# Second pass, last layer: sums loaded into a unit's own tile, split there and stored from it

## The chip, the cores and the metric

The kernel runs on one core of one Trainium2 chip. The metric is the time of one execution in microseconds (us) of device time. Three runs of the kernel before took 1361.62, 1360.89 and 1360.49 us, median 1360.89.

## The reference

The program is an attention without softmax, followed by two layers of dense products. For each of 8 batches and 8 heads it forms kv = kᵀv (64 by 64) over 576 rows, then q·kv, divides each row by its root mean square and multiplies it by a gain. The 4608 tokens by 512 features that come out go through

```
h = x @ w_in                               # 512 -> 2048
x = softplus(h) @ w_out                    # 2048 -> 512
h = max(x @ w1, x @ w2, x @ w3)            # three times 512 -> 768
out = h @ w2_out                           # 768 -> 512
```

Everything is float32.

## The kernel before

The tokens are worked on in five passes of 2 x 456 or 2 x 464 tokens (`NS`). A product in float32 is made of three float32r products (`mm3`, L153 to L157): operand and weight are each split into a high part (a cast) and a low part (the value less the high part), and high·high, high·low and low·high are summed in PSUM. From the second pass on a block of products is multiplied by a seven-product scheme in the manner of Strassen and Winograd (`SLOT`, `ORDER`, products m = 1 to 7), for which sums and differences of weight blocks are needed. The first pass multiplies plainly; beside that it joins the raw weights, forms those sums on GpSimd, and stores what the later passes load. There are groups H (first layer), X (second), three times three groups for the third layer, and the last layer with 42 blocks of three matmuls (`OUT_SEQ`), e for the half of the output columns, m for the product, c for the chunk.

Weights come to TensorE as units: a tile `u` of 128 x 1024 (512 KB) that holds a high and a low half. There are `U_BUFS` = 4 such buffers, and 2 of half the size, `u3`. The first unit of a group has a buffer of its own, `ux` (`unit_tile` with `own`); from the third pass on there are two of these, used in turn by the count of the list `uxs`. A unit of the last layer serves four blocks, 12 matmuls; there are 11 (`OUT_UNITS`), the last half as big.

Not all units are split in the first pass. For the groups 23 and 24 (`LATE`) and for the last layer only the sums are stored. In the second pass, from 3 to 94 units of planned time after its start, 19 items (8 of the groups, 11 of the last layer) go one after the other through `load_sums` (a load of 256 KB into `st`, 2 buffers), `split_ahead` (ScalarE casts, GpSimd or VectorE subtracts, into `ahead` tiles, 4 buffers shared with k and v) and `keep_ahead` (two stores). Afterwards `load_unit` loads them as any other unit, in the second pass too.

The order of the work is set by planned times: `at(t, ...)` collects events, which are sorted by time and traced in this order; a planner then orders the engines' instructions. In the passes one and two, and around each start of a pass, `pinned` holds the order of the DMA queue of SyncE (SP, which issues all the loads and stores in question) to the order of the events. That queue works in order: a load that waits for its buffer holds up all that is behind it. `LEAD` = 10 is the planned time by which a unit is loaded ahead. One unit of planned time is about 1.25 us.

The attention of the next pass lies beside the third layer (`attention_beside`): k and v of a batch are loaded by `load_kv` for four pairs of heads. The first pass is opened by `OPENING`, a list written by hand in which the order on all engines is fixed: `r2.7` is the second refinement step of pair 7 (VectorE, it releases a PSUM bank), `jb.2.0` joins a weight (VectorE), `hc.0.1.1` casts an activation and `cc.1.0` a pair of weight blocks (both ScalarE).

Of the kernel before, what the change touches and what calls it, by code (L numbers as in the profile page):

```python
# [8 lines left out]
F32 = mybir.dt.float32  # L9
# [6 lines left out]
B, H, S, D = 8, 8, 576, 64  # L16
NT, DM, DFF, DF2 = B * S, H * D, 2048, 768
P = 128
# [25 lines left out]
LEAD = 10  # L44
# [5 lines left out]
ss.4:Y ra.0.1:cv LW.1.0 o.6:W rs.5 ja.0.1 xh.3 mm.7 t.5:p r1.5 LW.1.1 sq.6 jb.0.1 xl.3:p rs.4 r2.5 LW.2.0 ev.7:a  # L50
r1.4 o.7:X ra.1.0:cv t.4:p r3.5 rb.1.0 ss.6:Y wc.0.1:p sq.7 H.0.0.0:X r2.4 s1.0 rs.6 ja.1.0 ra.1.1:at t.6:p r1.6
ra.2.0:at wl.0.1:p jb.1.0 cc.0.1:a ss.7:Y rb.2.0 r2.6 LW.2.1 SA.0 wc.1.0:a cl.0.1 ja.2.0 H.0.1.0:Y rs.7 r3.4
wl.1.0:p xh.5 SB.0 t.7:a jb.2.0 SC.0.1 xh.4 r2.7 LW.8.0 tab wc.2.0:p r1.7 H.1.0.0:Y r3.6 SA.1 ra.2.1:cv wl.2.0:p
r3.7 sp.0.0.0 xh.6 xl.5:v hc.0.0.0:a xl.4:p H.2.0.0:X xh.7 hl.0.0.0 rb.2.1 xl.7:p s2.0 s3.0 SA.2 xl.6:v sp.0.1.0
rb.8.0 ja.2.1 s4.0 H.0.0.1:X hc.0.1.0:a jb.2.1 sp.2.0.0 cc.0.2:p rb.1.1 hl.0.1.0 cl.0.2 LW.8.1 hc.2.0.0:a ja.1.1
H.2.0.1:Y ra.8.0:cv hl.2.0.0 cc.0.0:p sp.0.0.1 ja.8.0 SC.0.2 cl.0.0 sp.1.0.0 jb.1.1 LW.9.0 hc.0.0.1:a hc.1.0.0:v
ra.8.1:at s1.1 H.1.0.1:X jb.8.0 LW.9.1 wc.1.1:a cc.1.1:a hl.1.0.0 wl.1.1:p SC.0.0 sp.2.0.1 hl.0.0.1 rb.8.1
cl.1.1 H.0.1.1:X hc.2.0.1:a ja.8.1 sp.1.0.1 s2.1 hl.2.0.1 wc.2.1:a SB.1 jb.8.1 s3.1 hc.1.0.1:a SC.1.1 wl.2.1:v
wc.8.1:a H.1.1.1:Y s4.1 cc.1.0:a wl.8.1:v sp.0.1.1 cl.1.0 cc.1.2:a hl.1.0.1 hc.0.1.1:a SB.2 cl.1.2 s1.2 s2.2
s3.2 s4.2 s1.8 s2.8 s3.8 s4.8 H.2.1.0:X hl.0.1.1 sp.1.1.1 SB.8 hc.1.1.1:v SC.1.0 hl.1.1.1 H.1.1.0:X SC.1.2  # L60
sp.2.1.0 ra.9.0:cv rb.9.0 hc.2.1.0:v hl.2.1.0 ja.9.0 jb.9.0 H.2.1.1:X sp.1.1.0 ra.9.1:W wc.8.0:a hc.1.1.0:v
hl.1.1.0 wl.8.0:v sp.2.1.1 rb.9.1 hc.2.1.1:v hl.2.1.1 ja.9.1 jb.9.1 SA.8
# [5 lines left out]
def kernel(  # L68
# [12 lines left out]
    nc = tc.nc  # L81
# [50 lines left out]
    for s in range(2):  # L132
        hi = const.tile([P, NP, P], F32R, name=f"kvh{s}")
        lo = const.tile([P, NP, P], F32R, name=f"kvl{s}")
        kvs.append((hi, lo))

    def cast(eng, hi, src):
        if eng is nc.scalar:
            nc.scalar.copy(hi, src)  # L139
        else:  # L140
            eng.tensor_copy(hi, src)  # L141

    def split(eng_hi, src, hi, lo, eng_lo):
        cast(eng_hi, hi, src)
        eng_lo.tensor_tensor(out=lo, in0=src, in1=hi.bitcast(F32), op=ALU.subtract)  # L145
# [34 lines left out]
    def at(t, fn, *args):  # L180
        events.append((t, len(events), fn, args))
# [11 lines left out]
    wd, units, st = {}, {}, {}  # L193
    uxs = []

    def unit_tile(size, p, own=False):
        if own and "ge" in pools:
            uxs.append(pools["ux"] if "ux" in pools and len(uxs) % 2 else pools["ge"])
            return uxs[-1].tile([P, 2, 512], F32R, tag="ux", bufs=1, name="ux")
        if size == 2:  # L200
            return up.tile([P, 2, 512], F32R, tag="u", bufs=U_BUFS, name="u")
        return up.tile([P, 1, 512], F32R, tag="u3", bufs=U3_BUFS, name="u3")

    def keep(key, u):
        n = u.shape[1] * 512
        wd[key] = dr.tile([P, n], F32, tag=f"wd{len(wd)}", name=f"wd{len(wd)}")
        nc.sync.dma_start(out=wd[key], in_=u.rearrange("p i n -> p (i n)").bitcast(F32))
# [13 lines left out]
    def load_sums(key, c0, n):  # L221
        t = pools["st"].tile([P, 512], F32, tag="st", bufs=2, name="st")
        st[key] = t[:, 0:n]
        nc.sync.dma_start(out=st[key], in_=wd["o" if key[0] == "o" else ("s", key[0])][:, c0:c0 + n])

    staged = {}

# [6 lines left out]
        staged[key] = (hi, lo)  # L234

    def keep_ahead(key, size):
        n, i = 256 * size, 1 if key[0] == "o" else size
        hi, lo = staged.pop(key)
        wd[key] = dr.tile([P, 2 * n], F32, tag=f"wd{len(wd)}", name=f"wd{len(wd)}")
        dst = wd[key].rearrange("p (i h n) -> p i h n", i=i, h=2)  # L240
        for h, t in enumerate((hi, lo)):
            nc.sync.dma_start(out=dst[:, :, h], in_=t.rearrange("p (i n) -> p i n", i=i))
# [56 lines left out]
    OUT_UNITS = [(4 * i, min(4, len(OUT_SEQ) - 4 * i)) for i in range(-(-len(OUT_SEQ) // 4))]  # L299
# [383 lines left out]
    def new_batches(pas, t):  # L683

        a = TOK[pas] + t * NS[pas]
        first = -1 if a == 0 else (a - 1) // S
        return list(range(first + 1, (a + NS[pas] - 1) // S + 1))

    def attention_beside(pas, t0):

        n = NS[pas]

        for t, start in ((0, t0 - 2), (1, t0 + 25.1)):
            tile = gc_tile if t or pas == 1 else partial(ge_tile, pas - 1)
            for b in new_batches(pas, t):
                for p in range(NP):
                    at(start - (12.5, 11, 16, 14.5)[p], load_kv, b, p, False, tile if p > 1 else None)
                at(start, kv_mm, b)
                at(start + (1.25 if t else 0.1), kv_evict, b)
        for k in range(2 * NP):  # L700
            h, p = divmod(k, NP)
            a = TOK[pas] + h * n
            t = t0 + 8 + 6 * k
            at(t - (12 if pas == 1 else 6 if k else 10), load_q, a, n, p)
            at(t - 3, split_q, a, n, p)
            at(t + 0.3, out_mm, a, n, p)
            at(t + 0.4, square, a, n, p)
            at(t + 4.8, ssq_mm, a, n, p, "W" if pas == 1 else "at")
            at(t + 4.9, root, a, n, p)
            at(t + (5.5 if pas == 1 else 4.9), norm, a, n, p)  # L710
# [3 lines left out]
    def run_pass(pas, base):  # L714
# [37 lines left out]
        start = {name: base + 7 * i for i, name in enumerate(order)}  # L752
# [8 lines left out]

        if pas == 1:
            ahead = [((g, k), 256 * PLACE[ms[0]], len(ms)) for g in range(LATE, G_O[0]) for k, ms in enumerate(UNITS)]
            ahead += [(("o", i // 4), i * P, n // 2) for i, n in OUT_UNITS]
            for i, (key, c0, size) in enumerate(ahead):
                t = base + 3 + 91 / len(ahead) * i
                at(t, load_sums, key, c0, 256 * size)
                at(t + 5, split_ahead, key, size)
                at(t + 8, keep_ahead, key, size)
# [26 lines left out]
        for fp in range(8):  # L796
            t = start[f"H{fp}"]
# [19 lines left out]
        for n in range(4):  # L817
            if pas == 0:
                for q in range(2):
                    t = start[f"X{n}{q}"]  # L820
# [10 lines left out]
            for q in range(2):  # L831
                t = start[f"X{n}{q}"]
# [58 lines left out]
        for k in range(9):  # L891
            fp, j = divmod(k, 3)
            t = base2 + 7 * k
# [16 lines left out]
        if pas + 1 < NPASS:  # L910
            attention_beside(pas + 1, base2)
            for s, ms in enumerate(STEPS):
                at(base3 + 5 + SLOT[ms[-1]] + 0.5, combine_x, pas + 1, (s,))
# [69 lines left out]
        t = base3 + 2.05  # L983
# [2 lines left out]
            return base3 + 23  # L986
        for i, n in OUT_UNITS:
            key, size, ti = ("o", i // 4), n // 2, t + 0.5 * i
            at(ti - (6 if i == 0 else LEAD), load_unit, pas, key, size, i == 0)
        for i, b in enumerate(OUT_SEQ):  # L990
            at(t + 0.5 * i, out_block, *b)
# [113 lines left out]
    for n, step in enumerate(OPENING):  # L1105
        name, _, opt = step.partition(":")
        kind, *index = name.split(".")
        t = OPEN + 0.25 * n
# [12 lines left out]
    base, bases = 0, []  # L1121
    for pas in range(NPASS):
        bases.append(base)
        base = run_pass(pas, base)
# [105 lines left out]
```

## Time and profile before

| | us |
|---|---|
| runs, median (range) | 1360.89 (1360.49 to 1361.62) |
| the profiled execution | 1361.93 |
| its span, first to last instruction | 1360.1 |
| TensorE (PE) busy in it | 1348.6 |
| VectorE, ScalarE, GpSimd busy | 819.0, 735.8, 650.9 |

The execution is 1.8 us longer than its span; that part lies outside the instructions. Times in the trace count from the span's start. PE, DVE, ACT, POOL and SPq are TensorE, VectorE, ScalarE, GpSimd and SyncE's queue; PEld are weight loads. Matmuls overlap, so that a duration of 0.37 us stands beside a distance from start to start of 0.21 us.

### The profile page before, as it was taken

The page shows a single profiled execution, that of the slowest core. Times are in us where ns is not written, and L with a number is a line of the kernel's source. Part 1 is how long each engine was busy: PE and PEld are TensorE (multiplying, and loading weights), DVE is VectorE, ACT ScalarE, POOL GpSimd, SP SyncE. Part 2 cuts the span into 40 slices and gives each one's busy share as a digit, 9 for nine tenths or more (in the row PEclk, how much of TensorE's full clock was granted, in tenths as well). Part 3 has the DMA queues.
Part 4 walks back from the last instruction along what each step waited for, and adds up shares of the span by engine and source line. Part 5 has one row for each costly group of instructions (what it writes and reads, how often), then busy time and mean ns, then how long its engine had stood idle before and what let it go on. Part 6 is the DMA issues. An engine that isn't in the chain of part 4 may idle for free.

```text
span 1360.1 us, 20399 instructions
## 1 busy us (share of the span) xinstructions
PE 1348.6 (99%) x6956; PEld 1196.6 (88%) x6956; DVE 819.0 (60%) x1301; ACT 735.8 (54%) x1426; POOL 650.9 (48%) x612
## 2 busy tenths in 40 slices
PE   9999999999999999999999999999999999999998
PEld 6899999998888888888888888888889889998897
DVE  6856758883545767735555676445567754447544
ACT  6776657873755456456444564554356546443332
POOL 6866545665554534345335354444434444336320
PEclk9999999999999999999999999999999999999999
DMA  8799889777999776586678765766766576666665
GB/s 294 240 324 348 263 299 342 260 251 239 330 318 313 253 283 238 183 306 209 203 240 274 239 207 189 279 208 205 245 199 213 175 282 217 216 213 190 226 200 172
DMA packets 135543, 336.12 MB, mean 247 GB/s; under 512 B 14608, under 2 KB 41104, under 8 KB 135440
## 3 DMA queue, kind: packets, MB, share of 16 engines
q1 hardware_dynamic: 134864, 333.90, 72.9%
q8 instruction: 56, 0.92, 0.3%
q10 hardware_dynamic: 576, 0.92, 0.2%
q14 instruction: 47, 0.39, 0.1%
HBM read 269.35 MB, written 65.40 MB: 246 GB/s over the span
## 4 chain that ended last, share of the span: by engine, by line
PE 95%; DMA 2%; DVE 1%; ACT 1%; POOL 1%; issue 0%; SPq 0%; POOLq 0%; ACTq 0%
PE Xo L155 6%; PE Xo L156 6%; PE Xo L157 6%; PE Xx L155 5%; PE Xx L157 5%; PE Xx L156 5%; PE Xh L155 5%; PE Xh L157 5%; PE Xh L156 5%; PE Yo L155 3%; PE Yo L156 3%; PE Yo L157 3%; PE Yx L155 3%; PE Yx L156 3%; PE Yx L157 3%; PE Yh L155 3%
## 5 line engine op out<-in xcount | busy, mean ns | idle before, releaser
L145 POOL TENSOR_TENSOR lo<-e,hi 128x464 fp32r<-128x464 f32 (+1 forms) x160 | 188.8, 1213 | 174.8 <-ACT hi L139 161.0
L139 ACT CAST hi<-t 128x464 fp32r<-128x464 f32 (+1 forms) x120 | 65.6, 547 | 124.5 <-DVE e L151 50.5
L155 PE MATMUL Xo<-hi,u 128*128 128x464 f32 (+1 forms) x296 | 110.8, 376 | 0.5 <-ACT m L139 0.4
L156 PE MATMUL Xo<-lo,u 128*128 128x464 f32 (+1 forms) x296 | 109.9, 371 | 0.0
L157 PE MATMUL Xo<-hi,u 128*128 128x464 f32 (+1 forms) x296 | 109.7, 371 | 0.0
L148 DVE TENSOR_TENSOR x<-x,Xx 128x464 f32<-128x464 f32 (+1 forms) x104 | 65.6, 632 | 60.1 <-PE Xx L157 59.8
L155 PE MATMUL Xh<-hi,u 128*128 128x464 f32 (+1 forms) x266 | 99.7, 375 | 1.4 <-DVE h L141 0.7
L157 PE MATMUL Xh<-hi,u 128*128 128x464 f32 (+1 forms) x266 | 98.8, 371 | 0.0
L156 PE MATMUL Xh<-lo,u 128*128 128x464 f32 (+1 forms) x266 | 98.6, 371 | 0.0
L139 ACT CAST hi<-e 128x464 fp32r<-128x464 f32 (+1 forms) x160 | 86.4, 580 | 22.0 <-PE Yx L156 16.7
L139 ACT COPY m<-Xo 128x464 f32<-128x464 f32 (+1 forms) x108 | 58.6, 547 | 70.1 <-PE Xo L157 67.6
L145 DVE TENSOR_TENSOR lo<-t,hi 128x464 fp32r<-128x464 f32 (+1 forms) x120 | 75.9, 636 | 33.3 <-ACT hi L139 29.0
L155 PE MATMUL Xx<-hi,u 128*128 128x464 f32 (+1 forms) x256 | 95.4, 372 | 0.1
L157 PE MATMUL Xx<-hi,u 128*128 128x464 f32 (+1 forms) x256 | 95.0, 371 | 0.0
L156 PE MATMUL Xx<-lo,u 128*128 128x464 f32 (+1 forms) x256 | 94.8, 370 | 0.0
L151 POOL TENSOR_TENSOR e<-e 128x464 f32<-128x464 f32 (+1 forms) x32 | 38.1, 1191 | 107.1 <-DVE t L151 89.7
L145 POOL TENSOR_TENSOR u<-sw,u 128x256 fp32r<-128x256 f32 (+1 forms) x67 | 67.8, 1027 | 32.8 <-ACT u L139 27.8
L145 POOL TENSOR_TENSOR lo<-m,hi 128x464 fp32r<-128x464 f32 (+1 forms) x40 | 47.8, 1213 | 74.6 <-ACT hi L139 74.6
L139 ACT CAST u<-sw 128x512 fp32r<-128x512 f32 (+1 forms) x120 | 62.8, 540 | 37.6 <-POOL sw L151 17.1
L148 DVE TENSOR_TENSOR Wh<-h,Wh 128x464 f32<-128x464 f32 (+1 forms) x32 | 20.6, 644 | 95.6 <-PE Wh L157 79.9
L151 POOL TENSOR_TENSOR sw<-sw 128x256 f32<-128x256 f32 x84 | 66.7, 797 | 23.7 <-DVE sw L280 19.6
L663 POOL TENSOR_TENSOR og<-og,r 128x464 f32<-128x464 f32 (+1 forms) x32 | 40.4, 1263 | 68.7 <-DVE r L659 48.1
(260 smaller groups left out, 4100.6 us busy)
## 6 DMA issues: line engine op xcount, KB each, us to landing
u<-wd SPq DMA_DIRECT2D x241, 512.0 KB, 4.4
ux<-wd SPq DMA_DIRECT2D x99, 512.0 KB, 3.5
wd<-u SPq DMA_DIRECT2D x161, 256.0 KB, 4.8
u<-wd SPq DMA_DIRECT2D x104, 256.0 KB, 4.0
raw<-in_w_out_dram SPq DMA_DIRECT2D x22, 512.0 KB, 4.9
raw<-in_w_dram SPq DMA_DIRECT2D x18, 512.0 KB, 5.5
raw<-in_w_in_dram SPq DMA_DIRECT2D x16, 512.0 KB, 5.5
wd<-ahead SPq DMA_DIRECT2D x32, 256.0 KB, 6.0
```

The costliest lines, as they stand in the source:

```text
L139: nc.scalar.copy(hi, src)
L145: eng_lo.tensor_tensor(out=lo, in0=src, in1=hi.bitcast(F32), op=ALU.subtract)
L148: eng.tensor_tensor(out=o, in0=a, in1=b, op=ALU.add)
L151: eng.tensor_tensor(out=o, in0=a, in1=b, op=ALU.subtract)
L155: nc.tensor.matmul(acc, wh, xh, start=first, stop=False, skip_group_check=on)
L156: nc.tensor.matmul(acc, wh, xl, start=False, stop=False, skip_group_check=on)
L157: nc.tensor.matmul(acc, wl, xh, start=False, stop=last, skip_group_check=on)
L663: nc.gpsimd.tensor_tensor(out=og, in0=og, in1=r, op=ALU.mult)
```

## The change

Three things are edited. First, the 11 items of the last layer leave the list that is split ahead in the second pass; the 8 that stay are spread over the planned times 14 to 82 of the pass. In the last layer of the second pass each unit is now made on the spot: `load_whole` loads 256 KB of sums into the low half of the unit's own `u` tile, `split_whole` casts them into the high half (ScalarE) and subtracts in place (GpSimd), TensorE multiplies from it, and `keep` stores it (512 KB) for the later passes. The first unit of that layer no longer uses `ux`. Second, k and v of the pairs 0 and 1 for the second half of the third pass are loaded 11.5 and 12.5 units of planned time earlier. Third, two steps of the opening stand earlier in the list: `r2.7` ahead of `jb.2.0`, `hc.0.1.1` ahead of `cc.1.0`.

```diff
-wl.1.0:p xh.5 SB.0 t.7:a jb.2.0 SC.0.1 xh.4 r2.7 LW.8.0 tab wc.2.0:p r1.7 ...
+wl.1.0:p xh.5 SB.0 t.7:a r2.7 jb.2.0 SC.0.1 xh.4 LW.8.0 tab wc.2.0:p r1.7 ...
-wc.8.1:a H.1.1.1:Y s4.1 cc.1.0:a wl.8.1:v sp.0.1.1 cl.1.0 cc.1.2:a hl.1.0.1 hc.0.1.1:a SB.2 ...
+wc.8.1:a H.1.1.1:Y s4.1 wl.8.1:v sp.0.1.1 hc.0.1.1:a cc.1.0:a cl.1.0 cc.1.2:a hl.1.0.1 SB.2 ...
-    def keep(key, u):
+    def keep(key):
+        u = units[1, key]
         n = u.shape[1] * 512
         wd[key] = dr.tile([P, n], F32, tag=f"wd{len(wd)}", name=f"wd{len(wd)}")
         nc.sync.dma_start(out=wd[key], in_=u.rearrange("p i n -> p (i n)").bitcast(F32))
+    def halves(key):
+        u = units[1, key].rearrange("p i n -> p (i n)")
+        n = u.shape[1] // 2
+        return u[:, 0:n], u[:, n:2 * n]
+
+    def load_whole(key, c0, size):
+        units[1, key] = unit_tile(size, 1)
+        low = halves(key)[1]
+        nc.sync.dma_start(out=low.bitcast(F32), in_=wd["o"][:, c0:c0 + 256 * size])
+
+    def split_whole(key):
+        hi, lo = halves(key)
+        split(nc.scalar, lo.bitcast(F32), hi, lo, nc.gpsimd)
-                    at(start - (12.5, 11, 16, 14.5)[p], load_kv, b, p, False, tile if p > 1 else None)
+                    lead = ((24, 23.5) if pas == 2 and t else (12.5, 11)) + (16, 14.5)
+                    at(start - lead[p], load_kv, b, p, False, tile if p > 1 else None)
-            ahead += [(("o", i // 4), i * P, n // 2) for i, n in OUT_UNITS]
             for i, (key, c0, size) in enumerate(ahead):
-                t = base + 3 + 91 / len(ahead) * i
+                t = base + 14 + 68 / len(ahead) * i
         for i, n in OUT_UNITS:
             key, size, ti = ("o", i // 4), n // 2, t + 0.5 * i
+            if pas == 1:
+                at(ti - LEAD, load_whole, key, i * P, size)
+                at(ti - 4.5, split_whole, key)
+                at(ti - 2.5, keep, key)
+                continue
             at(ti - (6 if i == 0 else LEAD), load_unit, pas, key, size, i == 0)
```

## Rows read from the trace of the kernel before

**Rows 1.** The page: busy time of TensorE and weight loads, share of the span, instructions.
```profile
PE 1348.6 (99%) x6956; PEld 1196.6 (88%) x6956; DVE 819.0 (60%) x1301; ACT 735.8 (54%) x1426; POOL 650.9 (48%) x612
```
**Rows 2.** Stretches: length, busy time (instructions) of PE, PEld, DVE, ACT, POOL; clock, DMA, GB/s.
```profile
324.90:468.20 143.30, 140.29 (x661) 122.91 (x660) 75.58 (x122) 73.81 (x140) 73.90 (x62) 1.00 0.92 315
468.20:560.20 92.00, 91.83 (x500) 80.07 (x499) 64.74 (x102) 56.46 (x108) 42.72 (x34) 1.00 0.69 245
560.20:589.20 29.00, 29.00 (x139) 25.82 (x138) 18.62 (x31) 13.58 (x27) 12.75 (x11) 1.00 0.65 225
589.20:727.90 138.70, 138.70 (x662) 124.02 (x662) 69.66 (x113) 63.91 (x121) 59.29 (x51) 1.00 0.71 237
```
**Rows 3.** TensorE's waits, whole execution: what waited for what, us, times, longest.
```profile
PE Xx L155 <- DMA ux<-wd: 1.8, 1, 1.8
PE Yh L155 <- DVE t L618: 1.2, 1, 1.2
```
**Rows 4.** Timeline, second pass, TensorE's longest wait and the load that ended it.
```profile
450.50 0.45 PE L155 MATMUL Xx<-hi,ux 128*128 128x464 f32 x1 [1.84 <-DMA ux<-wd]
...
444.68 0.32 SPq L211 DMA_DIRECT2D ux<-wd  x1
```
**Rows 5.** DMA issues, 330 to 440 us: count, size of each, median time to landing.
```profile
u<-wd SPq DMA_DIRECT2D x26, 512.0 KB, 6.6
wd<-ahead SPq DMA_DIRECT2D x30, 256.0 KB, 5.9
```
**Rows 6.** Instructions on `ahead` tiles: count, ns min/median/max, first and last start.
```profile
L139 ACT CAST ahead<-st x19: 406/615/627, 336.0 to 446.7; 128x512 fp32r<-128x512 f32 x16, 128x256 fp32r<-128x256 f32 x3
L145 POOL TENSOR_TENSOR ahead<-st,ahead x10: 750/1296/1304, 336.7 to 447.2; 128x512 fp32r<-128x512 f32 x9, 128x256 fp32r<-128x256 f32 x1
```
**Rows 7.** Timeline, last layer of the second pass: a unit's load, unit 9, next pass.
```profile
562.57 0.32 SPq L211 DMA_DIRECT2D u<-wd  x1
...
585.48 0.37 PE L155 MATMUL Yy<-hi,u 128*128 128x464 f32 x1
...
589.24 0.37 PE L155 MATMUL Xh<-hi,ux 128*128 128x464 f32 x1
```
**Rows 8.** Timeline of SyncE's queue: two loads, nothing else under way.
```profile
504.08 0.32 SPq L211 DMA_DIRECT2D ux<-wd  x1
504.45 0.42 SPq L211 DMA_DIRECT2D u<-wd  x1
```
**Rows 9.** DMA issues, 504.0 to 504.7 us: the same two, time to landing.
```profile
ux<-wd SPq DMA_DIRECT2D x1, 512.0 KB, 3.2
u<-wd SPq DMA_DIRECT2D x1, 256.0 KB, 3.5
```
**Rows 10.** DMA issues at 30.0 and 30.4, at 76.4, and at 549.9 us.
```profile
raw<-in_w_in_dram SPq DMA_DIRECT2D x1, 512.0 KB, 4.1
wd<-u SPq DMA_DIRECT2D x1, 256.0 KB, 4.3
...
wd<-u SPq DMA_DIRECT2D x1, 256.0 KB, 2.1
...
u<-wd SPq DMA_DIRECT2D x1, 256.0 KB, 2.7
```
**Rows 11.** Timeline, start of the third pass: loads of `ux`, and group H1's first matmul.
```profile
584.00 0.49 SPq L211 DMA_DIRECT2D ux<-wd  x1
...
591.96 0.33 SPq L211 DMA_DIRECT2D ux<-wd  x1
...
595.57 0.37 PE L155 MATMUL Xh<-hi,ux 128*128 128x464 f32 x1
```
**Rows 12.** Timeline, opening: the VectorE step r2.7, and two ScalarE casts of weights.
```profile
33.91 0.62 DVE L618 SCALAR_TENSOR_TENSOR t<-ss,t 128x456 f32<-128x456 f32 x1
...
53.43 0.62 ACT L139 CAST u<-sw 128x512 fp32r<-128x512 f32 x1 [2.31 <-DMA wd<-u]
...
60.59 0.62 ACT L139 CAST u<-sw 128x512 fp32r<-128x512 f32 x1 [0.74 <-DMA wd<-u]
```

More of the change, by code (lines that the diff above doesn't have):

```diff
@@ L52 @@
 ra.2.0:at wl.0.1:p jb.1.0 cc.0.1:a ss.7:Y rb.2.0 r2.6 LW.2.1 SA.0 wc.1.0:a cl.0.1 ja.2.0 H.0.1.0:Y rs.7 r3.4
-wl.1.0:p xh.5 SB.0 t.7:a jb.2.0 SC.0.1 xh.4 r2.7 LW.8.0 tab wc.2.0:p r1.7 H.1.0.0:Y r3.6 SA.1 ra.2.1:cv wl.2.0:p
+wl.1.0:p xh.5 SB.0 t.7:a r2.7 jb.2.0 SC.0.1 xh.4 LW.8.0 tab wc.2.0:p r1.7 H.1.0.0:Y r3.6 SA.1 ra.2.1:cv wl.2.0:p
 r3.7 sp.0.0.0 xh.6 xl.5:v hc.0.0.0:a xl.4:p H.2.0.0:X xh.7 hl.0.0.0 rb.2.1 xl.7:p s2.0 s3.0 SA.2 xl.6:v sp.0.1.0
@@ L58 @@
 cl.1.1 H.0.1.1:X hc.2.0.1:a ja.8.1 sp.1.0.1 s2.1 hl.2.0.1 wc.2.1:a SB.1 jb.8.1 s3.1 hc.1.0.1:a SC.1.1 wl.2.1:v
-wc.8.1:a H.1.1.1:Y s4.1 cc.1.0:a wl.8.1:v sp.0.1.1 cl.1.0 cc.1.2:a hl.1.0.1 hc.0.1.1:a SB.2 cl.1.2 s1.2 s2.2
+wc.8.1:a H.1.1.1:Y s4.1 wl.8.1:v sp.0.1.1 hc.0.1.1:a cc.1.0:a cl.1.0 cc.1.2:a hl.1.0.1 SB.2 cl.1.2 s1.2 s2.2
 s3.2 s4.2 s1.8 s2.8 s3.8 s4.8 H.2.1.0:X hl.0.1.1 sp.1.1.1 SB.8 hc.1.1.1:v SC.1.0 hl.1.1.1 H.1.1.0:X SC.1.2
@@ L223, in load_sums @@
         st[key] = t[:, 0:n]
-        nc.sync.dma_start(out=st[key], in_=wd["o" if key[0] == "o" else ("s", key[0])][:, c0:c0 + n])
+        nc.sync.dma_start(out=st[key], in_=wd["s", key[0]][:, c0:c0 + n])
+    def halves(key):
[9 more added lines that the diff above has]
+        split(nc.scalar, lo.bitcast(F32), hi, lo, nc.gpsimd)
     staged = {}
@@ L236, in keep_ahead @@
     def keep_ahead(key, size):
-        n, i = 256 * size, 1 if key[0] == "o" else size
+        n, i = 256 * size, size
         hi, lo = staged.pop(key)
```

## The prediction

> **What bounds the kernel now.** I read the page's busy times first. TensorE is busy 1348.6 of 1360.1 us [rows 1], so only some 11 us of waiting can be won, plus whatever makes matmuls slow, and time is lost only where TensorE comes to wait. The list of TensorE's waits comes next: over a microsecond each are only a wait for the DMA of a `ux` unit, 1.8 us, and one for the VectorE step of line 618 (`refine2`), 1.2 us [rows 3]. Then the stretches. The H and X groups of the second pass take 143.3 us, those of the third 138.7, with the same matmuls (661 and 662 records) at the same granted clock of 1.00 [rows 2]. Of the 4.6 us between them 3.0 are idle time (143.30 less 140.29) and 1.6 are slower matmuls: 140.29/661 = 0.2122 us each against 138.70/662 = 0.2095. The DMA share is 0.92 against 0.71, and a 512 KB unit takes 6.6 us to land [rows 5]; alone it takes 3.2 [rows 9]. So this stretch is short of DMA. The last layer of the second pass has no idle time: 29.00 us for 139 matmuls, 0.2086 each [rows 2].
>
> **What the change takes away.** The 11 items of the last layer (the last half as big, so 10.5) leave the busy stretch. Each moved 256 KB in and 512 KB out, 8.3 MB in all; at 315 GB/s the stretch moves 45.1 MB, so 36.8 MB stay, in about 140 us 263 GB/s. That is two thirds of the way from 315 down to the 237 GB/s of the third pass, and I give the matmuls two thirds of their 1.6 us: 1.1 us. The 1.84 us wait at 448.7 ended when a `ux` load issued at 444.68 landed, 5.8 us later [rows 4]; at the emptier queue's 3.2 us it would be there before it is needed. With the slow first matmul behind it I take 1.9 us. The other 1.2 us of idle time are short waits for VectorE, of which the change removes little; I take nothing. Sum 3.0 us, with ends at 1.1 (the wait stays) and 4.6 (the stretch becomes like the third pass's). ScalarE's casts (0.62 us each) and half of the subtracts on GpSimd (1.30 us) [rows 6] leave too; both engines are busy half of the stretch, so that is worth nothing by itself.
>
> **The moved k and v loads** are four DMAs of SP's queue that now come ahead of a `u3` and some `u` loads and no longer meet those of the pairs 2 and 3. TensorE idles 92.00 less 91.83 = 0.17 us in that stretch [rows 2]. I take 0.1 gained; ends 0.5 lost (the loads behind them start later) and 0.3 gained.
>
> **The opening.** `r2.7` starts at 33.91, 0.60 us after the join that now follows it, so TensorE's 1.2 us wait shrinks by 0.6 [rows 3, 12]. `hc.0.1.1` no longer queues behind a cast that waited 2.31 us for a store to land [rows 12]. But TensorE then only arrives earlier at group X00, whose weights are cast at 60.59, when another store has landed (0.74 us waited) [rows 12]. That store hangs on the cast at 53.43, this one on an earlier store; neither edit moves either. So I take 0; ends 0.7 lost (the join, 0.67 us later, delays GpSimd's cast of the same weights) and 1.2 gained.
>
> **What it adds: the last layer.** Now a unit must be loaded, split, used and stored in one of four buffers. Count the time of SP's queue. By the planned times the order there is load 3, keep 0, load 4, keep 1, load 5, and so on: keep k at 2.5 ahead of its unit's start, load k+4 at 2. Unit 0 now takes a `u` buffer, so load 3 is what was load 4: it goes when the group before frees its buffer, at 562.57 [rows 7]. Keep 0 goes right behind it. Load 4 needs the buffer that keep 0 reads, so it waits until keep 0 has landed; keep 1 stands behind load 4 although its data has long been ready; load 5 waits for keep 1. The queue is a chain of pairs: one load and one store landing per unit.
>
> The price of a pair: a load of 256 KB lands after 2.7 us [rows 10]. DMAs issued right behind each other land in order. The 256 KB load issued 0.37 us behind a 512 KB one landed 3.5 + 0.37 - 3.2 = 0.65 us after it [rows 8, 9], and a 256 KB store behind a 512 KB load landed 4.3 us after its issue, alone 2.1 [rows 10]. So a 512 KB store should land 2 x 0.65 = 1.3 us after the load ahead of it: 2.7 + 1.3 = 4.0 us from load to load. TensorE uses a unit in 12 x 0.2086 = 2.5 us, so from the time the slack is gone each unit is 1.5 us late.
>
> Load 9 is the sixth after load 3: 562.57 + 6 x 4.0 = 586.6. Then 2.7 us to land, 0.62 for the cast, 1.30 for the subtract [rows 6], 0.15 for three hand-overs, less 0.42, since two matmuls with the high half go first: 4.35 us, ready at 590.9. Unit 9 started at 585.48 [rows 7]. The lag grows with each unit, so this is the whole loss: 5.4 us. From below: a 512 KB store that keeps to itself lands after 2.1 + 0.65 = 2.75 us; with 0.4 of issue the pair is 3.15, load 9 at 581.5, ready at 585.8: 0.3 us. From above: at the busy stretch's 5.9 us for a store [rows 5] a pair is 6.3 us, load 9 at 600.4 and the loss 19 us; nothing else is on the queue here (the DMA share was 0.65), so I keep 8 as the upper end.
>
> The Trainium skill has a rule here that speaks against the change: two DMAs through one queue are not ordered, and the issuing engine has to wait for the first one's semaphore (DMA: Bandwidth & Descriptors, section Two DMAs through the same engine are not ordered), so load 4 cannot ride behind keep 0. The same page (Anatomy of one DMA) gives, for the GpSimd path, about 2.0 us plus bytes/436 GB/s per DMA and says that the confirmed write weighs most where the target is HBM. An estimate from it: 3.2 us for the store, 3.6 per pair, a loss near 3.0 us. The rows disagree with its second half: a 256 KB store lands in 2.1 us, a load of that size in 2.7 [rows 10].
>
> **What follows in the third pass.** Its first `ux` load stood in the queue ahead of group H1's; now keeps 6 to 10 stand between, and it starts some 9 us later, about when TensorE needs it: 0.3 us. Then the count of `uxs`: unit 0 no longer adds to it, so H1's unit falls on the buffer that H0 uses. It was loaded at 584.00; now it waits until H0's first unit is used up, the time at which the load of H2 went, 591.96, and H1's first matmul came at 595.57 [rows 11]. That leaves 3.6 us for a load that takes 3.2 alone [rows 9] and 6.6 in a full queue [rows 5]: 0 to 3.0 us lost, and I take 0.5. Together 0.8.
>
> **The sum.** 5.4 + 0.8 lost, 3.0 + 0.1 gained: 3.1 us slower. The profiled execution took 1361.93, so 1365.0 there; it lies 1.0 above the median of 1360.89, to which the same 3.1 us are added: 1364.0.
>
> **Rivals.** *The ring keeps up* (the other side): each store lands on its own time and SP never binds, which is the lower end above: 0.3 lost there, 3.1 gained, 2.8 faster, 1358.1. For it speaks that the last layer's DMA share is only 0.65 and GpSimd's 0.44 [rows 2]; against it the order of landings [rows 8 to 10]. It decides where the loss falls under 3.1 us: a pair under 3.6 us, a store that lands within 3.2 us of its issue. *The engines' own order adds to it:* casts and subtracts stand in ScalarE's and GpSimd's queues behind, or ahead of, the last layer's copies out of PSUM and the next pass's splits, or H1's unit comes 3 us late; some 3.5 us more, 7 slower, 1367.5. For it: GpSimd had 12.75 of 29 us of work there and gets 14 us more. Against: most of that time it was free. *The relief does not come:* TensorE's wait at 448.7 stays, because the 8 items that stay meet the `ux` load elsewhere, and only 1.1 us is gained: 5 slower, 1366.0. Against: the load landed in a queue that loses a sixth of its bytes.
>
> **Chances.** The forecast has 0.45, with a range of its own from 1362.3 to 1366.0; the ring that keeps up 0.25, the engines' order 0.18, no relief 0.12. A measurement of this kernel can tell some 0.2%, 2.7 us, from no change, so slower begins at 1363.6 and faster at 1358.2. The forecast lies above 1363.6 in three fifths of its cases, 0.27, and within in 0.18. The ring that keeps up straddles the other bound: 0.14 faster, 0.11 within. The other two are slower but for 0.06. Faster 0.14, within 0.35, slower 0.51. The range of 8 in 10 goes from 1358.6 to 1367.8: it cuts off the half of the ring's rival that is fastest and the tail of the engines' order.
>
> **What would show it.** In the trace after, SP's queue in the last layer of the second pass should alternate load, store at 4.0 us per pair, with the load's wait put down to the DMA of the store; TensorE should idle about 1.5 us ahead of each of the units 7, 8 and 9, and not ahead of units 0 to 5. H and X of the second pass should take 140.3 us with a DMA share near 0.8 and no wait for `ux`. The opening should still reach group X00 at the time of a cast released by a store. The prediction is wrong if pairs come every 3.2 us or less, or if that stretch shortens by more than 4 us.

## Result: 1.3% slower, and the profile after

| | time, us (median; least to most) | profiled execution (span) |
|---|---|---|
| before | 1360.93 (1360.49 to 1361.62), 4 runs | 1361.93 (1360.1) |
| after | 1379.29 (1377.89 to 1379.73), 4 runs | 1379.73 (1377.9) |

The ratio is 1.0134, with a 95% interval from 1.0121 to 1.0146: 18.4 us slower. Forecast were 3.1 us; the measured time lies far above the range. The line of the page that answers to [rows 1]:

```profile
PE 1356.7 (98%) x6956; PEld 1201.2 (87%) x6956; DVE 817.6 (59%) x1296; ACT 735.0 (53%) x1426; POOL 657.5 (48%) x617
```

TensorE is busy 8.1 us longer with the same 6956 matmuls, and idle 9.7 us longer (21.2 against 11.5). The four stretches of [rows 2], taken from the same first matmul to the same last one (the fourth ends one matmul later), say where:

```profile
327.40:467.60 140.20, 139.43 (x661) 123.64 (x660) 70.92 (x117) 67.58 (x129) 66.01 (x56) 1.00 0.78 265
467.60:560.60 93.00, 92.17 (x500) 80.11 (x498) 64.98 (x102) 57.46 (x110) 44.50 (x36) 1.00 0.68 229
560.60:606.04 45.44, 35.76 (x140) 28.57 (x138) 21.32 (x31) 18.19 (x36) 25.83 (x21) 0.89 0.62 208
606.04:745.96 139.92, 139.19 (x663) 124.01 (x661) 68.89 (x114) 64.02 (x121) 58.79 (x50) 1.00 0.75 243
```

H and X of the second pass are 3.1 us shorter (140.26 from first matmul to first matmul, against 143.38), the attention stretch is 1.0 longer, the last layer 16.4 longer (45.44 against 29.03), H and X of the third pass 1.1 longer. That makes 15.4 us. The gain in H and X need not be all the change's: in run f2_lead below, which leaves these groups as they were, they took 142.08. Another 2.5 us stand ahead of all this, at the start of the profiled execution; profiles of the same stretch vary by as much with the opening unchanged (run f2_lead below: 2.3 us), so I read nothing from them. In the third row the clock is 0.89: the only stretch where it isn't 1.00.

Next the waits, first TensorE's and then those of SyncE's queue in the last layer (us in total, times, longest):

```profile
PE Xy L157 <- POOL u L145: 5.2, 4, 2.0
PE Xy L155 <- ACT u L139: 2.9, 3, 1.7
PE Yy L155 <- ACT u L139: 1.2, 1, 1.2
PE Yy L157 <- POOL u L145: 0.5, 1, 0.5
```
```profile
SPq L235 <- DMA wd<-u: 21.0, 6, 3.7
```

TensorE waits nine times, 9.8 us, for casts and subtracts of units; none of these lines is in [rows 3]. SyncE's queue waits six times, 21 us, to issue a load (line 235), and each time for the landing of the store ahead of it. (Behind load 9 two stores wait besides for a subtract, 7.3 us.) The timeline of that queue (L235 issues the loads, L208 the stores) has the pattern:

```profile
562.96 0.32 SPq L235 DMA_DIRECT2D u<-wo  x1
563.38 0.39 SPq L208 DMA_DIRECT2D wd<-u  x1
567.39 0.32 SPq L235 DMA_DIRECT2D u<-wo  x1
567.76 0.42 SPq L208 DMA_DIRECT2D wd<-u  x1
...
589.02 0.32 SPq L235 DMA_DIRECT2D u<-wo  x1
```

From unit 3's load to unit 9's are six pairs, (589.02 - 562.96)/6 = 4.34 us each. The DMA issues of 562 to 594 us give the two parts: 3.0 us for the load, and 3.9 us for a store that is issued 0.4 behind it. So a pair lasts until its store has landed, 0.4 + 3.9 us.

```profile
wd<-u SPq DMA_DIRECT2D x8, 512.0 KB, 3.9
u<-wo SPq DMA_DIRECT2D x7, 256.0 KB, 3.0
```

Then look at ScalarE's timeline (in brackets: idle time before, and what ended it), and at GpSimd's:

```profile
585.03 0.62 ACT L139 CAST u<-u 128x512 fp32r<-128x512 f32 x1
585.55 1.54 ACT L139 CAST hi<-og 128x464 fp32r<-128x464 f32 x3
590.28 0.55 ACT L139 COPY o<-Xy 128x464 f32<-128x464 f32 x1 [3.20 <-PE Xy L157]
590.72 1.06 ACT L139 CAST hi<-og 128x464 fp32r<-128x464 f32 x2
591.68 0.62 ACT L139 CAST u<-u 128x512 fp32r<-128x512 f32 x1
596.00 0.55 ACT L936 COPY o<-Xy 128x464 f32<-128x464 f32 x1 [3.70 <-PE Xy L157]
598.74 0.55 ACT L936 COPY o<-Xy 128x464 f32<-128x464 f32 x1 [2.19 <-PE Xy L157]
599.18 0.93 ACT L139 CAST u<-u 128x512 fp32r<-128x512 f32 x2
```
```profile
588.24 5.70 POOL L145 TENSOR_TENSOR lo<-og,hi 128x464 fp32r<-128x464 f32 x5
593.90 1.25 POOL L145 TENSOR_TENSOR u<-u 128x512 fp32r<-128x512 f32 x1
599.88 1.97 POOL L145 TENSOR_TENSOR u<-u 128x512 fp32r<-128x512 f32 x2 [4.72 <-ACT u L139]
```

Units 7, 8 and 9 (loads at 580.55, 584.83 and 589.02) landed 2.96, 2.89 and 2.99 us after their issues, at 583.51, 587.72 and 592.01. Their casts, the `u<-u` lines at 585.03, 591.68 and 599.18, start 1.5, 4.0 and 7.2 us later. Unit 8's stands behind a copy out of PSUM that waits for matmuls of unit 7, unit 9's behind two that wait for unit 8; unit 8's subtract stands besides behind five splits of the third pass's input, 5.7 us of work. So from unit 7 on there is a loop: a late unit makes its copy late, the copy makes the next cast late, the cast the next unit.

Last, TensorE itself after such a wait, and the clock (the last three columns: granted clock, DMA share, GB/s) ahead of the first fall and around two of the three:

```profile
595.21 0.75 PE L157 MATMUL Xy<-hi,u 128*128 128x464 f32 x1 [1.96 <-POOL u L145]
595.76 0.59 PE L156 MATMUL Xy<-lo,u 128*128 128x464 f32 x1
596.15 0.59 PE L157 MATMUL Xy<-hi,u 128*128 128x464 f32 x1
```
```profile
576.00:588.00 12.00, 6.73 (x27) 4.38 (x25) 6.69 (x12) 6.88 (x14) 8.24 (x7) 1.00 0.57 186
...
588.30:591.50 3.20, 3.17 (x9) 2.73 (x9) 0.64 (x1) 1.22 (x3) 3.20 (x3) 0.53 0.47 121
592.90:595.20 2.30, 0.36 (x2) 0.00 (x0) 0.00 (x0) 0.00 (x0) 2.26 (x2) 0.90 1.09 402
595.20:598.40 3.20, 3.19 (x9) 2.71 (x9) 0.00 (x0) 0.55 (x1) 0.00 (x0) 0.54 0.99 355
```

Matmuls start 0.387 us apart instead of 0.208 (595.76 and 596.15 above); the granted clock is 0.53 and 0.54 in these two stretches, the lower level, 1.2 GHz, for most of each. From 588.33 to 591.47, 595.21 to 598.34 and 601.53 to 604.96 there are 25 steps in 9.70 us; at 0.2086 they take 5.22. So 4.5 of the 16.4 us are slow matmuls, which the page counts as busy time, and 11.9 are waits and restarts. The Trainium skill (TensorE: Matmul & The Clock Gate, section Part 1: The HAM clock gate) gives columns divided by 1.2 GHz as the distance of matmuls at the lower level, an estimate of 387 ns for 464 columns; the trace agrees. For the upper level its formula gives an estimate of 196 ns; here it is 208.

### The profile page after: what moved, and what is told of

Read it like the earlier page. It is cut to its first block, busy times and chain, and to the rows that moved or that the text cites. A ratio compares the mean times of both kernels' runs of the same rounds, so it can differ in the third digit from the quotient of the medians.

```text
span 1377.9 us, 20364 instructions
## 1 busy us (share of the span) xinstructions
PE 1356.7 (98%) x6956; PEld 1201.2 (87%) x6956; DVE 817.6 (59%) x1296; ACT 735.0 (53%) x1426; POOL 657.5 (48%) x617
## 4 chain that ended last, share of the span: by engine, by line
PE 93%; POOL 2%; DMA 1%; DVE 1%; ACT 1%; issue 1%; SPq 0%; POOLq 0%; DVEq 0%; ACTq 0%
PE Xo L155 6%; PE Xo L157 5%; PE Xo L156 5%; PE Xx L157 5%; PE Xx L155 5%; PE Xx L156 5%; PE Xh L155 5%; PE Xh L157 5%; PE Xh L156 5%; PE Yo L155 3%; PE Yo L156 3%; PE Yo L157 3%; PE Yx L155 3%; PE Yx L156 3%; PE Yx L157 3%; PE Yh L155 3%
```

## Experiments

Two theories. PAIRS: SyncE's chain of load and store landings sets the pace. ORDER: the casts' and subtracts' places in their engines' queues set it. Times are compared with runs of the kernel before on the same chip, whose medians lay between 1360.75 and 1362.05. The table gives the four stretches of each profile, in us, each from its first matmul to the next one's (the fourth to one matmul later). They are single profiles: H and X, untouched in f2_lead and f3_opening, differ by up to 1.3 us there from the profile before.

| kernel | H, X | attention | last layer | third H, X | median, us | ratio to before, 95% |
|---|---|---|---|---|---|---|
| before | 143.38 | 91.96 | 29.03 | 138.84 | | |
| after | 140.26 | 92.99 | 45.44 | 139.92 | 1379.29 | 1.0121 to 1.0146 |
| e1_nosplit | 140.67 | 93.01 | 36.92 | 141.58 | 1371.02 | 1.0063 to 1.0090 |
| e2_nokeep | 140.79 | 93.00 | 30.35 | 139.44 | 1362.06 | 1.0000 to 1.0018 |
| e3_noring | 140.77 | 93.01 | 29.03 | 138.74 | 1359.52 | 0.9981 to 0.9998 |
| e5_early | 140.44 | 93.01 | 30.81 | 140.94 | 1363.31 | 1.0012 to 1.0031 |
| f1_parity | 140.69 | 93.02 | 30.75 | 140.10 | 1362.42 | 1.0003 to 1.0021 |
| f2_lead | 142.08 | 92.74 | 29.01 | 138.84 | 1361.77 | 1.0000 to 1.0018 |
| f3_opening | 143.09 | 92.15 | 29.00 | 138.88 | 1361.20 | 0.9989 to 1.0006 |
| f4_poolq | 140.88 | 92.30 | 32.10 | 138.74 | 1361.27 | 0.9988 to 1.0006 |
| e4_dve | 140.97 | 93.00 | 38.88 | 140.60 | 1372.25 | 1.0060 to 1.0088 |
| g1_half | 140.63 | 93.01 | 38.59 | 139.92 | 1370.18 | 1.0046 to 1.0074 |
| c3_hybrid | 140.83 | 92.28 | 30.73 | 138.74 | 1360.32 | 0.9983 to 1.0001 |
| h1_hybrid5 | 142.55 | 91.88 | 29.08 | 138.74 | 1359.66 | 0.9980 to 0.9998 |

**e1_nosplit**: the split left out; `keep_low` stores the loaded half twice, 512 KB. (Not shown: its definition, and the lines by which both products read the loaded half.)

```diff
-                at(ti - 4.5, split_whole, key)
-                at(ti - 2.5, keep, key)
+                at(ti - 2.5, keep_low, key)
```

> The last layer of the second pass without its split: a unit is loaded (256 KB) and stored (512 KB, the loaded half twice) as in the changed kernel, but cast and subtract are left out and both products read the loaded half (so the last layer computes with other numbers). Theory PAIRS (SP's queue, one load and one store landing per unit, sets the pace; the engines only add the time of a split): the pairs stay at 4.4 us, the load of unit 9 still lands near 592.0 and TensorE can then use it at once, against 585.9 without loss: 6 to 8 us lost in the stretch (16.4 in the changed kernel), about 1370 in all. Theory ORDER (the pace is set by the loop matmul, copy out of PSUM, cast, subtract, matmul, since casts and subtracts stand behind copies in ScalarE's and GpSimd's queues; SP's chain only starts it): without casts the loop is open and nearly all of the loss goes: 1363 to 1365.

1371.0. The pairs stayed, at 4.1 us each, and TensorE's waits in the last layer were for loads alone, 3.9 us, and at its end for H0's `ux` load, which stood behind the late stores:

```profile
PE Xh L155 <- DMA ux<-wd: 3.0, 1, 3.0
PE Xy L155 <- DMA u<-wo: 2.5, 2, 1.4
PE Yy L155 <- DMA u<-wo: 1.4, 1, 1.4
```
```profile
SPq L235 <- DMA wd<-u: 18.7, 6, 3.2
```

7.9 us were lost in the stretch, in the range that PAIRS gave; but 3.0 of it are the late `ux` load, which I had not counted there. The split and its place are worth the other 8.5.

**e2_nokeep** (the line of `keep` taken out), **e3_noring** (its neighbours `load_whole` and `split_whole` too).

> The changed kernel without the 11 stores of the last layer; the third pass loads other finished units of the same size in their place (its last layer computes with other weights). Loads and splits stay. PAIRS: with no store between them the loads follow the release of buffers, one per unit, and land long before use: under 2 us of the 16.4 stay, 1361 to 1364. ORDER: casts still stand behind copies that wait for TensorE, so waits ahead of the units 7 to 9 stay: at least half of the loss, 1371 or more.

> The changed kernel with nothing of the new last layer: both passes load other finished units (512 KB each, as before the change), no split and no store there (the last layer of both passes computes with other weights). What is left are the relief of the H and X groups, the moved k and v loads and the opening edits. By the profiles, at the same matmul, against the kernel before: H and X 3.3 us shorter, the attention stretch 0.7 us longer, H1's load no longer late. If the 2.4 us by which the opening came later in the profile are chance: 1358 to 1359. If they belong to the opening edits: 1360 to 1361. If the relief is chance: over 1361.

e2: 1.3 us are lost, TensorE waits for no cast or subtract (once, 0.9 us, for a copy on ScalarE), and loads wait only for buffers. So ORDER starts next to nothing by itself; it magnifies a lag that the pairs make. e3: without the new last layer the kernel is 0.1% faster than before, between the two ranges of the expectation: this is all that the relief is worth, less the attention stretch's loss.

**e5_early**: split and store earlier, so that SyncE's order is load, store k, load, store k+1 with each store a load ahead of the one that needs its buffer.

```diff
-                at(ti - 4.5, split_whole, key)
-                at(ti - 2.5, keep, key)
+                at(ti - 6.5, split_whole, key)
+                at(ti - 4.5, keep, key)
```

> The changed kernel with split and store of a unit two planned steps earlier (6.5 and 4.5 ahead of its unit instead of 4.5 and 2.5): the store of unit k now stands ahead of the load of unit k+3 on SP's queue and no load waits for the store right ahead of it, but for one issued a load earlier. PAIRS: two transfers are then in flight and the period falls from 4.4 to the 2.5 us that TensorE needs or near it; of the 16.4 us at most 5 stay, 1363 to 1368. ORDER: the waits behind copies stay, over 1373.

1363.3, and 1.8 us lost in the stretch. The loads now follow each other at TensorE's 2.5 us:

```profile
562.47 0.32 SPq L235 DMA_DIRECT2D u<-wo  x1
562.88 0.38 SPq L208 DMA_DIRECT2D wd<-u  x1
565.01 0.32 SPq L235 DMA_DIRECT2D u<-wo  x1
565.42 0.38 SPq L208 DMA_DIRECT2D wd<-u  x1
```

All bytes, loads, stores and splits are there; only their order changed, and 14.6 of the 16.4 us went. (ScalarE's order changed with it, since the program works out the engines' order anew; by itself this run doesn't tell SyncE's order from ScalarE's. e2, where the splits keep their planned times, does.)

**f1_parity** (e5_early and one dummy entry in `uxs`), **f2_lead** (before with the k and v loads moved), **f3_opening** (before with the two opening steps moved), **f4_poolq** (stores from GpSimd's queue, `uxs` and loads as before).

> The kernel of the earlier store (split and store 6.5 and 4.5 ahead) with the count of ux buffers put right: unit 0 of the last layer adds one entry, so H1's unit of the third pass again falls on the buffer that H0 does not use. In the run without this the profile shows a 1.95 us wait ahead of H1's first matmul with a ux unit. Theory COLLISION (that wait is the buffer that H0 holds): it goes, 2 us less than 1363.3, about 1361.3. Rival QUEUE (the load is late because stores and output stand ahead of it on SP's queue): the load is issued as late as before, 1363.

> The kernel before with the two pairs' k and v loads moved and nothing else. At the same matmul, five profiles of kernels that hold this edit lose 0.74 to 0.76 us in the attention stretch of the second pass. If this edit is the cause: 0.7 us slower than before, with a wait of 0.8 us ahead of an ss matmul near 485 and one of 0.3 near 497. If the cause is another one (the emptier H and X groups that reach this stretch earlier): no change there.

> The kernel before with the two opening steps moved and nothing else. The prediction took 0 (0.7 lost to 1.2 gained). Between the first k-v product and group X00 the profiles of five kernels with this edit are 0.5 to 1.6 us shorter than before, but the start of each varies by up to 2.8 us. If the edit earns this: 1 us faster, X00's first matmuls near 62.3 after an undisturbed start. If X00 hangs on the weights' store, as predicted: no change, within 0.3 us.

> The changed kernel with the stores of the last layer issued from GpSimd's queue right behind the subtract that they wait for, so that SP's queue holds loads alone; ux count put right, k and v loads back at their old place. PAIRS: the loads follow the release of buffers by stores that are issued as soon as the data is there; nothing of the 16.4 us is left but a wait under 1 us, H1's wait goes: 1358.5 to 1360.5. ORDER: casts behind copies keep the waits: over 1370. If issuing a DMA costs GpSimd more than a microsecond each, its subtracts become late: 1362 to 1366.

f1: 1.3 us above its runs of before, where e5 was 2.6 above its own, and 0.8 us less in the third pass, not 2: H1's wait for `ux` fell from 1.8 to 0.4, and another, for a `u`, of 0.5 came. Both theories seem to have a part. f2: the attention stretch grows by 0.8, with the two waits named, 0.62 and 0.21 us; the first is

```profile
487.99 0.47 PE L647 MATMUL ss<-sh,ones 128*128 128x464 f32 x1 [0.62 <-ACT sh L139]
```

No DMA is in this line. `sh` is a cast of the square of `o`, and ScalarE's timeline tells why it is late (first f2_lead, then the kernel before):

```profile
485.93 0.55 ACT L867 COPY m<-Xo 128x464 f32<-128x464 f32 x1 [1.62 <-PE Xo L157]
486.37 0.56 ACT L637 ACTIVATE sq<-o 128x464 f32<-128x464 f32 x1
...
487.35 0.59 ACT L139 CAST sh<-sq 128x464 fp32r<-128x464 f32 x1
```
```profile
483.20 0.58 ACT L139 CAST sh<-sq 128x464 fp32r<-128x464 f32 x1
483.69 0.55 ACT L139 COPY m<-Xo 128x464 f32<-128x464 f32 x1
484.93 0.55 ACT L866 COPY m<-Xo 128x464 f32<-128x464 f32 x1 [0.70 <-PE Xo L157]
```

In the kernel before the square starts at 480.90 and the cast at 483.20, ahead of that copy (its line is 866 there, 484.93); in f2_lead they stand behind it, and it waits for TensorE. With four loads moved, the program put ScalarE's steps in another order. f3: no change that can be measured. f4: SyncE's queue no longer alternates (it still waits three times, 7.5 us, for a store), yet 3.1 us are lost in the last layer and the time, 1361.27, lies above the range of PAIRS. TensorE waits 1.6 us there, 0.7 of it for a subtract and 0.6 for a copy on ScalarE; the rest is open.

**e4_dve**: both steps of the split on VectorE. **g1_half**: half of each store, the low half's 256 KB (the third pass's other loads are not shown).

```diff
-        split(nc.scalar, lo.bitcast(F32), hi, lo, nc.gpsimd)
+        split(nc.vector, lo.bitcast(F32), hi, lo, nc.vector)
```
```diff
-                at(ti - 2.5, keep, key)
+                at(ti - 2.5, keep_half, key)
```

> The changed kernel with both halves of the last layer's split on VectorE instead of ScalarE and GpSimd; SP's queue has the same order. What is asked is how much of the 16.4 us the engines' order adds to the pairs of SP. Without any split 9.1 us were lost there, so the split and its place cost 7.3. If that is mostly the place behind copies on ScalarE and the eviction's splits on GpSimd: on VectorE a unit is ready some 1.3 us after it lands, 10 to 11 us lost, 1372 to 1374. If any in-order engine does the same (VectorE has the other copies out of PSUM): no change, 1377 to 1380.

> The changed kernel with half of each store in the last layer left out (the low half alone is stored, 256 KB; the third pass loads other units there, so its last layer computes with other weights). Loads, splits and the order of SP's queue stay. PAIRS: a pair is shorter by the 0.65 us that 256 KB more add to a landing, 3.7 instead of 4.35 us; unit 9's load goes six pairs later than the first, so it lands 3.9 us earlier, and what hangs on the lag (waits behind copies, the lower clock) shrinks with it: 5 to 9 us lost in the stretch, 1367 to 1371. If a store's time is fixed and not its bytes': the pair stays over 4.2 us and the time over 1376.

e4: 6.6 of the 16.4 us go though SyncE's queue waits as long as in the changed kernel, so the place on ScalarE and GpSimd (and the lower clock that came of it) costs 6.6 us. A faster split is no rival for the units that were latest: on VectorE cast and subtract of the units 8 and 9 took 2.6 and 2.3 us, against 0.62 and 1.25, but the casts started 0.12 us after the loads had landed. Unit 9's cast there waits for its load alone:

```profile
SPq L235 <- DMA wd<-u: 21.3, 6, 3.8
```
```profile
592.67 0.78 DVE L141 CAST u<-u 128x512 fp32r<-128x512 f32 x1 [1.68 <-DMA u<-wo]
```

g1: five of the six pairs took 3.75 to 3.86 us, near the 3.7 expected, but one took 5.8, its store landing 5.3 us after its issue, for a reason left open; 9.6 us were lost, a little more than expected. A shorter store does shorten the pace.

**c3_hybrid** and **h1_hybrid5**: a part of the units split in place, with early stores, the others ahead (h1: `> 4` instead of `> 5`; the rest of the edit is told in the expectation).

```diff
+            ahead += [(("o", i // 4), i * P, n // 2) for i, n in OUT_UNITS if i // 4 > 5]
-                t = base + 14 + 68 / len(ahead) * i
+                t = base + 10 + 80 / len(ahead) * i
```

> A version that could beat both kernels: the last layer's units 0 to 5 are loaded as sums and split in place (split and store 6.5 and 4.5 ahead), the units 6 to 10 are split ahead during H and X as before the change; 13 items there, spread over the planned times 10 to 90; the ux count put right, k and v loads at their old place, the opening edits kept. H and X should keep about two thirds of the 3.3 us of relief, the last layer should lose under 0.5, as its lag grows only from the sixth unit on: 1358.5 to 1360, against 1360.9 before. If any unit split in place costs as much as in the kernel with all of them so: 1361 to 1362.

> The mixed version with five units split in place (0 to 4) and six split ahead (14 items in H and X). In the version with six, TensorE waited once, 1.4 us, for a copy out of PSUM on ScalarE; GpSimd's step of the combination stood there behind the subtract of unit 5, which waited for its load. If that place in GpSimd's queue is the cause, the wait goes with unit 5: 1.4 us less than the version with six, some 2.5 us under the kernel before of the same runs. If the wait comes from the order of ScalarE's copies alone, it stays and the time is that of the version with six, 1 us under before.

c3: 0.1% under before, the interval just reaches 1; the last layer lost 1.7 us, not under 0.5. TensorE's one wait, 1.3 us, is for a copy on ScalarE, which stood behind a cast that waited 3.9 us for VectorE's step of the combination (`og`). I had put that down to GpSimd's step of the combination, behind unit 5's subtract. The trace doesn't show it: VectorE was busy without a gap from 568.1 on, but one of its steps took 1.74 us instead of 0.63 while GpSimd did that subtract.

```profile
569.11 1.32 POOL L145 TENSOR_TENSOR u<-u 128x512 fp32r<-128x512 f32 x1 [2.15 <-ACT u L139]
```
```profile
569.19 1.74 DVE L145 TENSOR_TENSOR lo<-m,hi 128x464 fp32r<-128x464 f32 x1
```

With one unit fewer TensorE has no wait in the last layer (29.08 us), so unit 5's subtract has to do with it; how stays open. h1_hybrid5 is faster than the kernel before by 0.1%: ratio 0.9989, interval 0.9980 to 0.9998; 1.8 us, not the 2.5 expected, and about as much as c3 (1.7). Its relief in H and X is only 0.8 us (142.55), against 2.5 in c3: another wait, 1.1 us for VectorE, came there.

## Why the prediction was wrong, step by step

**H and X: right, in part by luck.** 3.1 us gained against 3.0; 140.26 us, as forecast 140.3, DMA share 0.78, no `ux` wait. 0.9 us of it are faster matmuls (1.1 forecast), 2.2 less waiting (1.9). The rival "the relief does not come" falls. But the 1.8 us wait belonged to one profile: in f2_lead and f3_opening, with all 19 items still there, TensorE waits 0.2 and 0.5 us for `ux` loads and the stretch takes 142.08 and 143.09. Against these two the gain is 1.8 and 2.8 us.

**Moved k and v loads: wrong in sign.** 0.1 gained was forecast, with 0.5 lost as the end; 0.8 (f2) to 1.0 us were lost. The step counted DMAs and SyncE's queue; what cost time was a new order on ScalarE.

**Opening: right in number**, no change (f3). The reason given is open: the cast of weights that stood at 60.59 waits 0.19 us for a store in the kernel after (62.76), but for none in f3, where it starts at 60.18, straight behind ScalarE's step before it.

**The chain of pairs: right in mechanism, short in size.** Alternating loads and stores, each load held by the store ahead of it: seen in six waits, and undone by e2 and e5. The Trainium skill's rule that a transfer needing an earlier one's end must wait for its semaphore (DMA: Bandwidth & Descriptors, Two DMAs through the same engine are not ordered) is what those six waits show. The 3.2 us for a store, the prediction's estimate from the Trainium skill (the same page, Anatomy of one DMA), were 3.9. A pair took 4.34 us, not 4.0: the store landed 1.3 us behind the load, as forecast, but the load took 3.0 us and not 2.7 (the two loads just ahead of the ring, with no store behind them, took 2.73). By the prediction's own working this makes unit 9 ready at 589.02 + 4.35 = 593.4, 7.5 us late, instead of 5.4.

**The step that failed** is the one from landing to use: "2.7 us to land, 0.62 for the cast, 1.30 for the subtract, 0.15 for three hand-overs". It takes both engines as free when the data lands. For unit 6 it was nearly right (load 576.15; the first matmul with the low half, due 4.35 + 0.42 us later, came at 581.85, 0.9 late). For the units 7, 8 and 9 that matmul came 3.0, 5.6 and 7.4 us later than the step allows, at 588.33, 595.21 and 601.22, since unit 8's cast came 4.0 and unit 9's 7.2 us after the landing. So the 16.4 us are 7.5 from the chain, 7.4 from landing to use (a part of it matmuls at the lower clock) and 1.5 behind that, again at the lower clock. The rival "the engines' own order adds to it" had this cause, at a chance of 0.18 and 3.5 us; it was 6.6 by e4. I set it low because the engines are half idle there; a queue whose head waits for TensorE is idle too, and blocks all the same. The waits began at unit 5, not 7.

**Not foreseen: the clock.** After these waits TensorE went on at 1.2 GHz three times, 4.5 us in all, a part of it within the 6.6. No term or rival had that. No run takes the clock by itself; the 4.5 are counted from the steps.

**Third pass: right in number by luck**, 1.1 us against 0.8, and not as told: no wait for `ux` came. H1's `ux` load was issued at 608.76 behind H0's release, but H1 began with another unit, and its first matmul waited for VectorE's copy out of PSUM.

```profile
612.14 0.37 PE L157 MATMUL Xh<-hi,u 128*128 128x464 f32 x1
613.25 0.47 PE L155 MATMUL Xh<-hi,u 128*128 128x464 f32 x1 [0.73 <-DVE h L141]
```

The stretches explain 15.4 of 18.4 us. The other 3 are open: 2.5 of them stand at the start of the profiled execution, which no edit explains (f3), and the same start varies from profile to profile by up to 3.9 us (323.5 to 327.4).

## What to carry to other kernels

In a ring that loads, works and stores in the same few buffers each unit lasts as long as its store takes to land (4.3 us here, where TensorE needs 2.5) when each load is queued right behind the store that frees its buffer, and the next store behind that load; splits and stores one load earlier gave back 14.6 of 16.4 us here with not a byte less. When a unit can come late, follow its work through the in-order queue of every engine it uses and ask what that queue's head waits for: an engine that is free on average isn't free if a copy that waits for TensorE stands in front. And where a program works out the engines' order, as here, a moved event can change the order on other engines too, not only on the queue it is issued from.

## What the hardware showed

The clock. TensorE had waited five times since 576, and had been busy 6.7 of 12 us at a granted clock of 1.00, when it went on at 588.33 at the lower level. In e1_nosplit three waits of 1.1 to 1.4 us for loads left it at the upper level; after the one of 3.0 us for `ux` it ran three matmuls and then fell. So a wait can cost more than its length: 7.5 us of lag from the pairs became 16.4 by this and by the loop through ScalarE and GpSimd.

A shorter period did not make the transfers slower: in e5_early there was a load and a store every 2.5 us at first, in the kernel after one of each every 4.34, and the loads landed in 3.1 and 3.0 us (medians), the stores in 3.9 in both.
